# A planned kernel's orders anew: linear attention and an MLP twice, on one Trainium2 core

## The chip, the cores and the metric

The kernel runs on one core of a Trainium2 chip. Its engines are TensorE (PE, matmuls; PEld its weight loads), VectorE (DVE), ScalarE (ACT), GpSimd (POOL) and SyncE (SP, which here issues DMAs). Each works through a queue of its own in order and waits on semaphores for the others. The metric is the device time of one execution in microseconds (us), the median of some runs; smaller is better.

## The reference

The input x has 2048 rows of 512. Two layers follow each other with the same weights, and each has two parts with a residual addition:

```
x = x + A(layernorm(x))        # linear attention, 32 heads of 16
x = x + B(layernorm(x))        # MLP, 512 -> 1792 -> 512
A(x): q, k, v = x @ wqkv;  phi(t) = where(t > 0, t + 1, exp(t)) + 1e-6
      kv = sum over rows of phi(k)^T v;  z = sum over rows of phi(k)
      out = (phi(q) kv) / (phi(q) z + 1e-6) @ wo
B(x): layernorm(x); gelu(y @ w1 + b1) @ w2 + b2
```

## The kernel before, in words

The 2048 rows are 16 tiles of 128, four to a chunk. A kernel function first lists every operation as a node of a graph (`G.op`, with its engine, a duration in ns, what it reads and writes, its buffers and its name), and then plays the nodes on five queues in an order that is written out by hand as strings in `CONF`: `ORDER` names every operation of each engine in order, `PLACES` says which buffer of a pool holds which tiles one after another, `WAY` chooses the engine or the form of single operations. The durations decide nothing at run time; what runs is set by the orders and the buffers. `Settled` turns `PLACES` into dependencies (a tile's first operation waits for all users of the tile before it in the buffer) and `assign_waits` turns dependencies into semaphore waits.

The names are needed to follow the steps. The number behind a name is layer, chunk, tile:

- `statsA0_4`, `aggr`, `veps`, `pow`, `nmr`, `norm` (L783 to L811): layer norm of tile 4 ahead of the attention part of layer 0 (`A0`), or the MLP (`B0`). VectorE takes statistics (L783, L785), `veps` adds the epsilon (L790, VectorE or GpSimd), GpSimd raises to the power -0.5 (`pow`, L792), `nmr` (L803, GpSimd) is needed if ScalarE normalizes (L806); else VectorE does (L811).
- `TA0_4`, `TB0_4`: the DMA transposition of a normalized tile, issued by SP (L820). `PTA0_2`, `PTC0`: the same on TensorE (L833), whose result `tc` copies from PSUM (L843).
- `K0_4`, `Q0_1_3`: key and query matmuls (L887, L908, L920). `exp`, `relu` (ScalarE, L855, L866), `min` (VectorE, L859, L868) and `phi` (L861, L872) make the feature map from the PSUM bank. The form called "max" needs no relu, but VectorE reads the bank.
- `G0_4_0` (L997, L1026): the sum of y^T phi(k), from which `KV` (L1047) and `M` (L1070) make one matrix per layer. `zaA5`, `za5` (L971) add up phi(k) over tiles for z; `Z`, `ZH`, `ZR` are small matmuls for z; `cpg`, `cpm`, `kvm`, `zb`, `dz` copies and masks on the way.
- `D`, `pz`, `red`, `den`, `rec`, `pr`: the division. Where a chunk is treated by token, `pz` (L1112) multiplies phi(q) by z's row, `red` (L1115) sums per head, `rec` (L1120) inverts, `pr` (L1124) scales, and `TP` (L1128) transposes by DMA. `pz` and `pr` run on VectorE or GpSimd.
- `WO` (L1141) and `RA` (L1146): output matmul and residual. `b2` (L1157): addition of the bias to the residual, VectorE or GpSimd.
- `W1` with `gelu` (L1171, L1176) and `W2` with `RB` (L1208, L1214, at the end L1218, L1194 and L1200 with the stores `OD`): the MLP. In each layer's first chunk `W1` is split in two halves of 256 columns (`W10_1_5_0`, `W10_1_5_1`).

The key operations run on one chunk after another; while the MLP of layer 0 runs, norms, keys and queries of layer 1 are made for the chunks that are ready. At the start TensorE is kept running by `warm` matmuls without use, x is loaded in chunks (`x0`, `x1`, `xc1`, `xc3`, `xc2`) by SP, and the weights that are needed later (`wv`, `wo`, `w1`, `w2`) by GpSimd's queue (L730). The choices that the change touches read so:

```
on_pool = eng(f"veps{tag}") != "dve"          # L787
on_pool = eng(f"pz{tag}") != "dve"            # L1110
on_pool = eng(f"pr{tag}") == "pool"           # L1122
on_pool = eng(f"b2{L}_{st}") != "dve"         # L1156
```

Of the kernel before, what the change touches and what calls it, by code (L numbers as in the profile page):

```python
# [12 lines left out]
D = 512  # L13
# [172 lines left out]
def assign_waits(graph, order, sems, dma_sems):  # L186
# [10 lines left out]
    while len(done) < total:  # L197
        moved = False
        for e in ENGINES:
# [1180 lines left out]
```

## Time and profile before

| | |
|---|---|
| median of 3 runs | 323.85 us (323.73 to 323.98) |
| profiled execution | 325.95 us, of which the span of its instructions is 324.7 us |
| mean granted TensorE clock in the span | 0.995 |
| matmuls' busy time | PE 317.4 us |
| VectorE, ScalarE, GpSimd busy | 224.4, 190.4, 148.0 us |
| GpSimd `pow` (L792) | 64 of them, mean 666 ns |
| GpSimd `veps` (L790), `nmr` (L803) | 32 at 268 ns, 28 at 375 ns |
| GpSimd `pr` (L1124), `pz` (L1112), `b2` (L1157) | 17 at 1133 ns, 14 at 1186 ns, 9 at 1225 ns |
| VectorE `veps` (L790), `pz` (L1112), `pr` (L1124), `b2` (L1157) | 31 at 139 ns, 10 at 766 ns, 7 at 976 ns, 23 at 705 ns |
| ScalarE table loads (L1334) | 13 at 1283 ns |

The rows for VectorE and GpSimd are from the view of groups of instructions. A group by tokens (L1124) stands apart from the division by feature (L1094: 6 on GpSimd at 1161 ns, 2 on VectorE at 687 ns). Instructions of one engine overlap by some tens of ns, so an instruction's step to the next one is shorter than its duration. In a timeline the columns are start, busy time, engine, line, operation, output and inputs, shape, count, and in brackets the idle time of the engine before it and what ended it. Busy digits are tenths of slices of 8.1 us.

### The profile page before, as it was taken

How to read it: one execution, taken by the hardware profiler on the slowest of the kernel's cores; microseconds unless marked ns; L12 is line 12 of the kernel's file. 1: busy time of each engine (PE TensorE's matmuls, PEld its weight loads, DVE VectorE, ACT ScalarE, POOL GpSimd, SP SyncE). 2: the span in 40 equal slices, each digit the busy share in tenths (PEclk: the TensorE clock that was granted, in tenths of full speed). 3: DMA queues.
4: the chain of work that ended last, by engine and by line, in shares of the span. 5: the costliest groups of instructions: out<-in, count | busy, mean ns of one | idle time of the engine just before them, and what ended most of it. 6: DMA issues, size and time to landing. Idle time of an engine off the chain costs nothing.

```text
span 324.7 us, 4679 instructions
## 1 busy us (share of the span) xinstructions
PE 317.4 (98%) x1649; PEld 157.3 (48%) x1679; DVE 224.4 (69%) x541; ACT 190.4 (59%) x324; POOL 148.0 (46%) x212
## 2 busy tenths in 40 slices
PE   6999999999999999999999999999999999999997
PEld 2443445567444444444444444558644444444444
DVE  4898889999797881327279799998998894000103
ACT  3898667597660446557953478878564441663220
POOL 4789778692806642302465324976564322000000
PEclk9899999999999999999999999999999999999999
DMA  7634299314103303012201110123044233100001
GB/s 255 181 68 81 49 358 260 67 33 88 27 16 65 68 15 81 18 33 48 19 16 32 32 34 0 27 58 68 0 82 67 48 85 108 34 0 32 18 32 65
DMA packets 52355, 21.68 MB, mean 67 GB/s; under 512 B 47532, under 2 KB 50860, under 8 KB 52332
## 3 DMA queue, kind: packets, MB, share of 16 engines
q1 hardware_dynamic: 50844, 16.37, 22.7%
q0 software_dynamic: 1056, 4.72, 3.9%
q10 hardware_dynamic: 432, 0.30, 0.3%
q8 instruction: 13, 0.21, 0.3%
q14 instruction: 10, 0.08, 0.1%
HBM read 8.00 MB, written 2.10 MB: 31 GB/s over the span
## 4 chain that ended last, share of the span: by engine, by line
PE 87%; POOL 5%; DVE 4%; DMA 2%; issue 1%; ACT 0%; SPq 0%
PE ps L1171 29%; PE ps L1208 28%; PE ps L1141 9%; PE ps L920 6%; PE ps L887 5%; PE ps L1026 4%; PE ps L997 2%; POOL rstd L792 2%; POOL zacc L971 1%; DMA t<-in_A_x_dram 1%; PE ps L908 1%; PE ps L1194 1%; POOL veps L790 1%; DVE stats L783 1%; DVE yb L811 1%
## 5 line engine op out<-in xcount | busy, mean ns | idle before, releaser
L1176 ACT ACTIVATE gT<-ps,b1c 128x512 bf16<-128x512 f32 (+1 forms) x140 | 77.5, 600 | 64.2 <-PE ps L1171 63.7
L1171 PE MATMUL ps<-t,w 128*128 128x512 bf16 (+1 forms) x549 | 101.2, 336 | 0.6
L1208 PE MATMUL ps<-w,gT 128*128 128x512 bf16 x427 | 97.7, 379 | 0.4
L1171 PEld LDWEIGHTS ps<-t,w 128*128 128x128 bf16 x560 | 54.7, 98 | 43.7 <-ACT gT L1176 0.4
L1208 PEld LDWEIGHTS ps<-w,gT 128*128 128x128 bf16 x434 | 42.4, 98 | 50.6
L792 POOL TENSOR_TENSOR rstd<-veps,neghalf 128x1 f32<-128x1 f32 x64 | 42.1, 666 | 23.2 <-DVE veps L790 19.2
L855 ACT ACTIVATE eb<-ps 128x512 bf16<-128x512 f32 x62 | 35.5, 604 | 20.8 <-PE ps L887 7.8
L887 PE MATMUL ps<-wqkv,t 128*128 128x512 bf16 x128 | 33.1, 390 | 2.8 <-ACT t L843 1.8
L1218 DVE TENSOR_TENSOR yb<-ps,xsb 128x512 bf16<-128x512 f32 x15 | 10.1, 687 | 35.8 <-PE ps L1208 35.8
L783 DVE BATCH_NORM_STATS2 stats<-xsb 128x6 f32<-128x512 f32 x48 | 32.3, 684 | 0.4
L1141 PE MATMUL ps<-gtb,t 128*128 128x512 bf16 x125 | 30.7, 379 | 0.2
L806 ACT ACTIVATE yb<-xsb,nmr,rstd 128x512 bf16<-128x512 f32 x21 | 17.1, 813 | 21.1 <-POOL nmr L803 16.7
L1124 POOL TENSOR_TENSOR t<-t,rr 128x512 bf16<-128x512 bf16 x17 | 19.1, 1133 | 22.2 <-DVE rr L1120 21.8
L1214 DVE TENSOR_TENSOR xsb<-ps,xsb 128x512 f32<-128x512 f32 x16 | 10.9, 684 | 21.8 <-PE ps L1208 21.7
L866 ACT ACTIVATE rb<-ps 128x512 bf16<-128x512 f32 x43 | 25.0, 606 | 1.3 <-PE ps L908 0.8
L790 POOL TENSOR_SCALAR veps<-mv 128x1 f32<-128x1 f32 x32 | 8.6, 268 | 35.8 <-DVE mv L785 28.2
L920 PE MATMUL ps<-wqkv,t 128*128 128x512 bf16 x94 | 23.9, 379 | 0.1
L887 PEld LDWEIGHTS ps<-wqkv,t 128*128 128x128 bf16 x128 | 12.4, 100 | 19.1 <-ACT t L843 2.6
L1157 DVE TENSOR_TENSOR xsb<-xsb,b2b 128x512 f32<-128x512 f32 x23 | 15.9, 705 | 7.1 <-ACT yb L806 7.1
L1112 POOL TENSOR_TENSOR lr<-t,zrow 128x512 f32<-128x512 bf16 x14 | 16.6, 1186 | 7.4 <-ACT zrow L1010 4.2
L1141 PEld LDWEIGHTS ps<-gtb,t 128*128 128x128 bf16 x128 | 12.5, 98 | 14.5 <-ACT gtb L1010 0.2
L811 DVE TENSOR_SCALAR yb<-xsb,mv,rstd 128x512 bf16<-128x512 f32 x27 | 15.0, 563 | 6.3 <-POOL rstd L792 5.7
(99 smaller groups left out, 375.6 us busy)
## 6 DMA issues: line engine op xcount, KB each, us to landing
w<-in_B_w_dram POOLq DMA_DIRECT2D x4, 896.0 KB, 11.1
out_dram<-yb SPq DMA_DIRECT2D x15, 128.0 KB, 2.0
t<-in_A_x_dram SPq DMA_DIRECT2D x3, 512.0 KB, 4.9
t<-yb SPq DMA_TRANSPOSE x62, 2.5
wqkv<-in_A_wqkv_dram SPq DMA_DIRECT2D x1, 512.0 KB, 5.9
wqkv<-in_A_wqkv_dram POOLq DMA_DIRECT2D x1, 512.0 KB, 7.2
wo<-in_A_wo_dram POOLq DMA_DIRECT2D x1, 512.0 KB, 7.8
t<-in_A_x_dram SPq DMA_DIRECT2D x1, 384.0 KB, 4.4
```

The source lines that it names most:

```text
L783: G.op("dve", lambda e: e.bn_stats(stats[:, s.slot, :], src()), 620, reads=src_keys, writes=[k + "s"], tiles=[s, *src_tiles], name=f"stats ...
L792: G.op("pool", lambda e: e.tensor_tensor(rstd[:, s.slot:s.slot + 1], veps[:, s.slot:s.slot + 1], neghalf[:], op=ALU.pow), 570, reads=[k + ...
L811: G.op("dve", lambda e: e.tensor_scalar(yb[:, y.slot, :], src(), mean(), rstd[:, s.slot:s.slot + 1], op0=ALU.add if by_act else ALU.subtra ...
L855: G.op("act", lambda e: e.activation(eb[:, et.slot, 0:n], bank(bt, n), ACT.Exp, scale=by()), 478 if n == D else 265, reads=[src_key, *more ...
L866: G.op("act", lambda e: e.activation(rb[:, rt.slot, 0:n], bank(bt, n), ACT.Relu, scale=by()), 478 if n == D else 265, reads=[src_key, *mor ...
L887: ins = e.matmul(bank(b), lhsT=yTa(yT)[:, dt, k * P:(k + 1) * P], rhs=wqkv[:, dt, D:2 * D], start=(i == 0 and n == 0), stop=(i == len(part ...
L920: ins = e.matmul(bank(b), lhsT=yTa(yT)[:, dt, k * P:(k + 1) * P], rhs=wqkv[:, dt, 0:D], start=(dt == 0), stop=(dt == DT - 1))
L1124: lambda e, d=d, tok=tok, heads=heads: e.tensor_tensor(heads(tok()), heads(tok()), rr[:, d.slot, :].unsqueeze(2).broadcast_to([P, H, DH]), ...
L1141: ins = e.matmul(bank(wb), lhsT=yTa(pq)[:, kt, k * P:(k + 1) * P], rhs=gtb[:, kt, :], start=(kt == 0), stop=(kt == DT - 1))
L1171: ins = e.matmul(bank(b, n), lhsT=w1[:, dt, ft * P:(ft + 1) * P], rhs=yTa(yT)[:, dt, k0 * P:k1 * P], start=(dt == 0), stop=(dt == DT - 1))
L1176: G.op("act", lambda e, ft=ft, b=b, k0=k0, k1=k1, n=n: e.activation(gT[:, g.slot, ft * 512 + k0 * P:ft * 512 + k1 * P], bank(b, n), ACT.Ge ...
L1208: ins = e.matmul(bank(b), lhsT=gT[:, g.slot, ft * 512 + k * P:ft * 512 + (k + 1) * P], rhs=w2[:, ft, :], start=(ft == 0), stop=(ft == FT - 1))
```

## The change

It rewrites most of the strings in `ORDER` and `PLACES` and 50 choices in `WAY`. The operations, their number and what they compute stay the same but for the engine of these 50:

- `veps`: 12 go from GpSimd to VectorE (A0_8, A0_11, A0_12, A0_13, A0_15, A1_0, A1_2, A1_14, B0_0, B0_6, B0_14, B1_12), 11 from VectorE to GpSimd (A0_1, A1_1, A1_4, A1_7, B0_1, B0_12, B1_0, B1_3, B1_5, B1_7, B1_10).
- `pr`: pr0_2_2, pr0_3_3, pr1_0_0, pr1_2_2, pr1_3_2, pr1_3_3 go to VectorE; pr0_1_0, pr1_2_0, pr1_2_1 to GpSimd. `pz`: pz0_3_1, pz0_3_3, pz1_3_3 go to VectorE; pz1_2_0, pz1_2_3, pz1_3_0 to GpSimd.
- `b2`: b20_0, b20_2, b20_8, b20_10, b21_1, b21_4 go to VectorE; b20_1, b20_5, b20_11, b21_5, b21_7 to GpSimd. zaA5 goes to GpSimd.

A new function `load_half` (half a tile of x by its own DMA) comes in, but no entry of `LOADS` calls it; the loads, the warm-up groups and the order of the chunks stay. The core of the diff, with the first lines of each queue:

```diff
         "sp":
-            "x0 x1 wka wkc xc1 wq xc3 TA0_0 TA0_1 xc2 TA0_4 TA0_5 TA0_7 TA0_6 TA0_15 TA0_12 TA0_13 TA0_8 TA0_14 TA0_10 TA0_11 "
-            "TA0_9 b1 b2 Tb1 TP0_0_3 TP0_0_1 TP0_0_0 TP0_0_2 TB0_4 TB0_5 TB0_6 TB0_7 TB0_3 TB0_2 TP0_2_1 TB0_1 TB0_0 TP0_2_2 "
...
+            "x0 x1 wka wkc xc1 wq xc3 TA0_0 xc2 TA0_1 TA0_4 TA0_5 TA0_7 TA0_6 TA0_15 TA0_13 TA0_12 TA0_14 TA0_8 TA0_10 TA0_11 "
+            "TA0_9 b1 b2 Tb1 TP0_0_3 TP0_0_1 TP0_0_0 TP0_0_2 TB0_4 TB0_5 TB0_7 TB0_6 TB0_3 TP0_2_1 TB0_0 TB0_1 TB0_2 TP0_2_2 "
+            "TP0_2_3 TP0_2_0 TA1_4 TP0_3_2 TP0_3_0 TP0_3_1 TB0_10 TP0_3_3 TB0_8 TB0_11 TB0_9 TB0_12 TA1_5 TB0_13 TB0_15 TA1_3 "
...
         "pe":
-            "warm0 warm6 warm8 warm7 warm4 warm5 PTC0 warm2 warm1 K0_0a warm3 K0_0b K0_0c PTC1 K0_0d PTA0_2 K0_1 K0_2 Q0_0_2 "
-            "PTA0_3 G0_0_0 K0_3 Q0_0_1 Q0_0_0 G0_1_0 K0_4 G0_2_0 K0_5 G0_3_0 K0_7 Q0_1_0 K0_6 Q0_1_3 Q0_1_2 G0_4_0 G0_5_0 "
-            "K0_12 K0_15 K0_13 G0_6_0 K0_14 K0_8 K0_10 K0_11 K0_9 G0_7_0 Z0_3 Q0_0_3 G0_12_0 Z0_2 ZHA Q0_1_1 G0_13_0 D0_1_2 "
...
+            "warm0 warm5 warm1 warm4 warm8 PTC0 warm2 warm6 warm3 warm7 K0_0a K0_0b PTC1 K0_0c K0_0d PTA0_2 K0_1 K0_2 Q0_0_2 "
+            "PTA0_3 G0_0_0 K0_3 Q0_0_0 Q0_0_1 G0_1_0 K0_4 G0_2_0 K0_5 G0_3_0 K0_7 Q0_1_3 K0_6 Q0_1_0 Q0_1_2 G0_4_0 G0_5_0 "
+            "G0_6_0 K0_12 K0_13 K0_15 K0_14 K0_8 K0_10 K0_11 K0_9 Q0_0_3 Q0_1_1 G0_7_0 Z0_3 Z0_2 ZHA G0_12_0 G0_13_0 D0_1_2 "
...
+            "W10_1_10_1 W10_1_5_1 W10_1_2_1 W10_0_4_0 W10_0_13_0 W10_1_8_1 W10_0_1_0 W10_0_10_0 W10_0_5_0 W10_0_2_0 W10_1_9_1 "
...
+            "W20_6_0 W20_6_7 W10_2_3_0 W10_2_5_0 K1_4 W10_2_11_0 W10_2_10_0 W10_2_1_0 W20_7_0 W10_2_2_0 W10_2_12_0 W20_7_7 "
...
         "act":
-            "wkb wkd sumA0_3 tcC0 sqA0_3 tcC1 tcA0_2 expk0_0 reluk0_0 expk0_1 expk0_2 reluk0_1 tcA0_3 reluq0_0_2 reluk0_2 "
-            "expk0_3 reluk0_3 expq0_0_1 normA0_7 expq0_0_2 reluq0_0_0 expk0_4 reluq0_0_1 normA0_15 expk0_5 normA0_13 reluk0_5 "
...
+            "wkb wkd sumA0_3 tcC0 sqA0_3 tcC1 expk0_0 tcA0_2 reluk0_0 reluk0_1 expk0_1 expk0_2 tcA0_3 expq0_0_2 reluk0_2 "
+            "reluq0_0_2 expk0_3 normA0_7 expq0_0_0 reluk0_3 reluq0_0_1 expq0_0_1 reluq0_0_0 normA0_15 expk0_4 expk0_5 "
...
+            "gelu0_0_8_0 gelu0_0_9_0 gelu0_0_3_0 gelu0_0_7_0 gelu0_0_12_0 normB0_11 normB0_9 gelu0_2_5_0 expk1_4 gelu0_2_11_0 "
...
         "dve":
-            "ones statsA0_0 aggrA0_0 cenA0_0 statsA0_2 aggrA0_2 statsA0_1 aggrA0_1 vepsA0_1 cenA0_1 normA0_2 normA0_0 "
-            "normA0_1 statsA0_4 statsA0_5 aggrA0_4 mink0_0 aggrA0_5 normA0_3 phik0_0 statsA0_7 mink0_1 aggrA0_7 mink0_2 "
...
+            "ones statsA0_0 aggrA0_0 cenA0_0 statsA0_2 statsA0_1 aggrA0_2 aggrA0_1 cenA0_1 normA0_0 normA0_2 statsA0_4 "
+            "statsA0_5 mink0_0 aggrA0_4 normA0_3 normA0_1 aggrA0_5 phik0_0 statsA0_7 normA0_4 aggrA0_7 statsA0_6 mink0_1 "
...
-            "aggrA0_11 statsA0_9 phik0_6 phiq0_1_0 zaA5 aggrA0_9 minq0_1_2 minq0_0_0 zaA6 mink0_12 minq0_1_3 phik0_12 "
...
+            "mink0_6 aggrA0_11 phiq0_0_0 phik0_6 vepsA0_11 statsA0_9 mink0_7 minq0_1_2 minq0_1_0 minq0_1_3 phiq0_1_2 aggrA0_9 "
+            "phiq0_1_0 phik0_7 mink0_12 zaA6 normA0_9 phik0_12 mink0_13 mink0_15 phik0_13 phiq0_1_3 mink0_14 zhiA phik0_15 "
+            "mink0_8 mink0_10 phik0_10 mink0_9 mink0_11 phik0_9 phik0_11 zloA zs0_3 zs0_2 zshA zb0 dz0 minq0_1_1 minq0_0_3 "
...
+            "statsB0_7 statsB0_6 aggrB0_7 RA0_0 RA0_2 statsB0_3 RA0_1 statsB0_0 aggrB0_3 aggrB0_0 aggrB0_6 vepsB0_3 red0_2_1 "
+            "vepsB0_6 statsB0_2 minq0_2_3 statsB0_1 vepsB0_0 aggrB0_2 aggrB0_1 normB0_7 red0_2_2 normB0_6 den0_2_1 phiq0_2_3 "
+            "den0_2_2 pz0_2_0 b20_3 rec0_2_1 pr0_2_1 pz0_2_3 minq0_3_3 rec0_2_2 normB0_0 red0_2_3 normB0_1 red0_2_0 phiq0_3_3 "
+            "b20_0 RB0_5 b20_7 den0_2_0 minq0_3_0 b20_6 den0_2_3 RA0_9 minq0_3_2 statsA1_5 pz0_3_3 minq0_3_1 phiq0_3_2 "
...
         "pool":
-            "id0 bdm0 id1 neghalf vepsA0_0 powA0_0 negA0_3 vepsA0_2 powA0_2 powA0_1 vepsA0_3 bdm1 powA0_3 vepsA0_4 vepsA0_5 "
-            "powA0_4 powA0_5 vepsA0_7 powA0_7 zaA1 nmrA0_7 vepsA0_15 vepsA0_6 powA0_6 powA0_15 vepsA0_13 zaA2 nmrA0_15 "
-            "powA0_13 nmrA0_13 zaA3 vepsA0_12 powA0_12 vepsA0_8 powA0_8 vepsA0_14 nmrA0_8 vepsA0_10 powA0_14 nmrA0_14 "
-            "powA0_10 zaA4 eps6 nmrA0_10 vepsA0_11 powA0_11 nmrA0_11 vepsA0_9 powA0_9 zaA7 phik0_14 phik0_8 b1z wv wo w1_0 "
...
+            "id0 bdm0 neghalf id1 bdm1 vepsA0_0 powA0_0 negA0_3 vepsA0_2 powA0_2 vepsA0_3 vepsA0_1 powA0_3 powA0_1 b1z "
+            "vepsA0_4 powA0_4 vepsA0_5 powA0_5 vepsA0_7 powA0_7 vepsA0_6 nmrA0_7 zaA1 powA0_6 powA0_15 powA0_13 nmrA0_15 zaA2 "
+            "nmrA0_13 zaA3 vepsA0_14 powA0_12 powA0_14 vepsA0_10 nmrA0_14 powA0_8 powA0_10 nmrA0_8 nmrA0_10 zaA4 powA0_11 "
+            "nmrA0_11 zaA5 vepsA0_9 powA0_9 zaA7 phik0_14 phik0_8 eps6 wv wo w1_0 w1_1 w2_0 w2_1 phiq0_1_1 pr0_1_0 pz0_0_0 "
+            "pr0_1_3 pz0_0_1 pr0_0_3 pz0_0_2 pr0_1_1 pr0_0_1 pr0_0_0 pr0_0_2 vepsB0_4 powB0_4 vepsB0_5 powB0_5 phiq0_2_2 "
...
     WAY={
...
-        "zaA2": "pool", "zaA5": "dve", "zaA6": "dve", "zc0": "0 1",
+        "zaA2": "pool", "zaA5": "pool", "zaA6": "dve", "zc0": "0 1",
...
+        def load_half(name, queue, h, after):
+            G.parts[("x0", 0)] = (("x0", 0, 0), ("x0", 0, 1))
+            ps_ = slice(64 * h, 64 * h + 64)
+            loaded[name] = dma(queue, lambda e: e.dma_start(
+                t4[ps_, x0[0].slot, 0:D].rearrange("p (k d) -> p k d", k=1), rows(x_dram, 0)[ps_, 0:1, :]),
+                [("x0", 0, h)], [x0[0]], name=name, kb=64, after=after)
+
         for name, queue, what, at, lo, hi, behind in cf["LOADS"]:
             after = [loaded[b] for b in behind.split()]
-            if what == "x":
+            if what == "half":
+                load_half(name, queue, at, after)
+            elif what == "x":
                 load_x(name, queue, at, lo, hi, after)
```

408 rows, old and new, of tables (ORDER, PLACES, WAY) are left out of this document.

## The prediction, made before the result

> **What bounds the kernel now.** The page's first part comes first.
>
> ```profile
> PE 317.4 (98%) x1649; PEld 157.3 (48%) x1679; DVE 224.4 (69%) x541; ACT 190.4 (59%) x324; POOL 148.0 (46%) x212
> PE   6999999999999999999999999999999999999997
> ```
>
> TensorE (PE) is busy in 98% of the span; a busy PE is not PE at its peak, so I read starts instead. In PE's timeline a row's start, its count and the next row's start give the pace:
>
> ```profile
> 26.85 2.75 PE L887 MATMUL ps<-wqkv,t 128*128 128x512 bf16 x12
> 29.44 1.03 PE L997 MATMUL ps<-pkb,yb 128*128 128x512 bf16 x4
> 31.09 3.83 PE L887 MATMUL ps<-wqkv,t 128*128 128x512 bf16 x16 [0.62 <-DVE pkb L861]
> 35.22 1.02 PE L887 MATMUL ps<-wqkv,t 128*128 128x512 bf16 x4 [0.30 <-DMA t<-yb]
> 36.08 1.03 PE L997 MATMUL ps<-pkb,yb 128*128 128x512 bf16 x3
> ```
>
> Twelve matmuls take 29.44 - 26.85 = 2.59, or 0.216 each, and a group of four 0.86. The four from 29.44 take 1.65 (0.79 lost), the sixteen from 31.09 take 4.13 (0.67 lost). I went through the whole timeline so, with 0.109 for 256 columns: from 37 us to the last matmul at 322.8 one loss shows, of 0.09 at 277 (jumps of 0.21, one matmul, are missing records). So behind 37 us nothing can be won on PE and any stall is pure loss; the tail behind 322.8 (last addition and store) keeps its operations. All gain lies before 37 us. There the first real matmul starts at 6.97, behind the landing of x1 at 5.68 and ScalarE's sum and copy, and runs slowly:
>
> ```profile
> 6.97 0.61 PE L887 MATMUL ps<-wqkv,t 128*128 128x512 bf16 x1 [1.79 <-ACT t L843]
> 7.58 1.06 PE L887 MATMUL ps<-wqkv,t 128*128 128x512 bf16 x2
> 8.43 0.64 PE L833 MATMUL ps<-idp,yb 128*128 128x128 bf16 x4
> 6.97:10.38 3.41, 3.41 (x15) 1.80 (x16) 3.07 (x10) 1.66 (x4) 3.04 (x7) 0.50 0.92 320
> ```
>
> The last of these is from the view by windows: the granted clock was 0.50 from 6.97 to 10.38, so two matmuls took 0.85 instead of 0.43. Waits from 6.97 on cost, by the same count, 0.17 ahead of K0_3 (14.08), 0.79 ahead of K0_14, 0.20 ahead of K0_11, 0.46 ahead of K0_9: 1.62 us, and the slow clock about 1.6.
>
> **The start, part by part.** The end of a row is the time at which an operation can release others; between engines a release costs PE 0.24 where it waited.
>
> The half clock stays, as I take it: K0_0a still waits for the same copy (6.91). Behind it the order is K0_0a K0_0b PTC1 K0_0c K0_0d, without warm3 (0.21) between. The transposition PTC1 then ends at 8.44 instead of 9.08, its copy tcC1 at 9.06 instead of 9.70. ScalarE now runs expk0_0 before tcA0_2, so mink0_0 starts on VectorE at 10.05 and not at 11.16, where DVE's timeline shows an idle 1.05 for it. normA0_3 follows at 10.4 to 10.8 (before 11.46 to 11.85), so PTA0_3, its copy and K0_3 can come at 13.8 instead of 14.08: 0.28 won.
>
> K0_14 waited for VectorE (phik0_12 ended 31.04), and VectorE waited for GpSimd:
>
> ```profile
> 27.82 0.70 DVE L971 TENSOR_TENSOR zacc<-zacc,pkb 128x512 f32<-128x512 f32 x1 [0.58 <-POOL eps L725]
> 26.63 1.16 POOL L971 TENSOR_TENSOR zacc<-zacc,pkb 128x512 f32<-128x512 f32 x1
> 27.81 0.77 POOL L803 TENSOR_SCALAR nmr<-mv,rstd 128x1 f32<-128x1 f32 x1
> 28.93 1.07 POOL L792 TENSOR_TENSOR rstd<-veps,neghalf 128x1 f32<-128x1 f32 x1
> ```
>
> The first row is zaA5, which the change moves to GpSimd: VectorE loses 0.63 (its steps lie that far apart) and the 0.58 of waiting, and gains five veps less one at about 0.1. GpSimd gains zaA5 (1.16) and loses four net veps with their gaps (4 x 0.28 = 1.12), so its load is even, but its chain of powers starts earlier: powA0_5 at 12.4 instead of 13.34, and, with the queue walked at 0.55 to 0.6 a power, powA0_11 at 26.3 instead of 30.00 and powA0_9 at 28.8 instead of 31.39. The transposes (1.27 to issue, 1.2 to land) then put K0_11's input at 30.8 (33.76) and K0_9's at 33.0 (35.08), against turns at 32.8 and 33.7. Walking VectorE's new queue from 10.05 (stats 0.62, min 0.21, phi 0.35 or 0.60 with PSUM, norm 0.35) gives phiq0_1_2 27.9, phiq0_1_0 28.6, phik0_12 31.1, phik0_11 36.7 (before 38.41), each ahead of the PE turn that needs its bank: K0_13 28.5, K0_15 29.4, K0_10 31.9. The nearest is K0_14 behind reluq0_1_3, 29.7 against 30.2. So all of the 0.17 + 0.79 + 0.20 + 0.46 can go; with a gain of 0.28 at K0_3 that holds the first 0.17, the sum is 0.28 + 1.45, **1.7 us**; my walk gives 46.93 for KV0_0, shown at 48.70, so 1.77. Below this, 0 is the bound: none goes if something else is late there.
>
> Other edits of the start cost nothing: bdm1 (0.92) goes into GpSimd's gap between 2.68 and 4.21; xc2 is issued before TA0_1, whose reader Q0_0_1 has 1.1 to spare; pr0_1_0 on GpSimd fits into the gap before pz0_0_0, which waited for it on VectorE until 45.93; the weight loads come earlier.
>
> **Behind the start** the stream must keep this lead. Work moves both ways. VectorE gets three pr net (0.68 to 1.59, quiet row 0.69) and one b2 (0.69), pz stays ten, veps shifts; GpSimd loses three pr (1.13) and one b2 (1.22). Of these two pr, two pz and one b2 fall between 48 and 120 us: 5 x 0.69 = 3.4 us more for VectorE, which by the view by windows sat idle there for 8.5 of 72 us, 1.4 of it before 80. The tight places by the queues:
>
> (a) W10_0_4_0 now comes at 79.5, where the first such matmul came at 82.10. It needs all four TB0_0 to TB0_3. The queue of SP runs TB0_7 TB0_6 TB0_3 TP0_2_1 TB0_0 TB0_1 TB0_2 at 1.27 each; VectorE's quiet rows put normB0_0 at 74.0 and normB0_1 at 75.2, so TB0_2 lands at 79.05, 0.45 ahead, of which 0.24 is the release. Six powers are in that chain; at the mean row 666 ns instead of the quiet 550 that is 0.70 late, less 0.2 to spare: 0.5. Ends: 0, if quiet; and, below, 3.0.
>
> (b) ScalarE loads its table 15 times behind the first instead of 13 (1.28 each). At K1_4 the chain gelu, load, exp, load, gelu is 0.02 + 0.69 + 1.31 + 0.60 + 1.31 + 0.69 + 0.24 = 4.86, against PE work of 4.97 until W10_2_2_0 needs the bank. I take 0, hidden by W20_7_0; up to 0.5 if PE's work were in another order.
>
> (c) pr1_0_0 on VectorE ahead of RA1_4 makes RA1_4 0.35 late; the matmuls of the next layer's up projection had 0.85 to spare, now 0.5: 0.
>
> Sum: 1.77 - 0.5 = 1.27. Against the profiled execution (span 324.7, time 325.95, so 1.25 outside) that is 323.4 and 324.7. The plain runs stand 2.1 below it (323.73 to 323.98); that offset is carried over: 323.85 - 1.27 = 322.58, **forecast 322.6**, alone 321.9 to 323.2.
>
> **Rivals.** *The lead is spent* (0.17): VectorE or GpSimd is late at (a) by 1.3 to 2.6, or the plain runs have less of the start's waits than the profiled one; 323.2 to 324.5, say 323.8. For it: VectorE is at 7.5 of 8 us in most of 48 to 80.
>
> *The port* (0.23), slower. GpSimd's power takes 0.55 in quiet rows, but:
>
> ```profile
> 70.44 1.98 POOL L792 TENSOR_TENSOR rstd<-veps,neghalf 128x1 f32<-128x1 f32 x1
> 70.72 0.69 DVE L1124 TENSOR_TENSOR t<-t,rr 128x512 bf16<-128x512 bf16 x1
> 71.32 0.69 DVE L1157 TENSOR_TENSOR xsb<-xsb,b2b 128x512 f32<-128x512 f32 x1
> ```
>
> The power was held while two additions or products of two SBUF tensors ran on VectorE; elsewhere such a product took 1.59 and a pz 1.52 instead of 0.69. The change puts four more of them on VectorE. If in chain (a) one power is held so (1.43), one pr (0.91) and one pz (0.84), TB0_2 is 3.18 late, 2.98 beyond what is to spare: more than the lead, 323.85 + 1.2 = 325.1. From 2.6 on it decides for slower. Against it: only one power of 64 took over 1.1. [...]
>
> *The clock* (0.05): the slow 6.97 to 10.38 goes. PE was busy for 1.45 of the 3.41 us before; two more warm-up groups before K0_0a add 0.22. It would give K0_1 0.9 earlier (PTC1 then waits for cenA0_1 at 7.65): 321.4 or so. [...]
>
> **Numbers.** Forecast 0.55, clock 0.05, lead spent 0.17, port 0.23. A measurement of this kernel can tell 0.2% (0.65 us) from no change: faster 0.60, same 0.17, slower 0.23. The range 321.8 to 325.1 leaves out the clock and half of the port.
>
> **What would show it.** In the changed trace K0_3 starts near 13.8, K0_14 to K0_9 run without a gap, KV0_0 starts near 46.9, W10_0_4_0 waits under 1 us for TB0_2, and nothing else stops PE. It is wrong if zaA6 or a phi holds K0_13 to K0_10, if a power over 1 us stands in chain (a), or if PE shows gaps beyond 85 us.

## The result, and the profile after

The changed kernel took 322.75 us (median of six runs, 322.25 to 323.22) beside 323.84 for the kernel before on the same chip: ratio 0.9963, 95% interval 0.9950 to 0.9976. Twelve more runs gave 323.26 (322.19 to 324.50) beside 323.89: 0.9977, 0.9964 to 0.9990. The forecast was 322.6. (A ratio is the comparison's own figure and not the quotient of the two medians.)

The first part of the page of after, and its row by slices:

```profile
PE 315.9 (98%) x1648; PEld 156.7 (49%) x1679; DVE 224.1 (70%) x545; ACT 191.8 (60%) x326; POOL 140.4 (44%) x208
PE   7999999999999999999999999999999999999997
```

GpSimd lost 7.6 us of busy time (148.0 to 140.4), VectorE's stayed (224.4 to 224.1), PE lost 1.5 (317.4 to 315.9), mostly its rows at half pace: the second profile of after, which has such rows, shows 317.0. The shares tell nothing of where the gain is. PE's timeline does, for the stretch that lost 1.62 us in before (lines are eight higher than there):

```profile
6.20 0.60 PE L895 MATMUL ps<-wqkv,t 128*128 128x512 bf16 x2 [0.82 <-ACT t L851]
...
23.09 2.75 PE L1005 MATMUL ps<-pkb,yb 128*128 128x512 bf16 x12
25.68 7.34 PE L895 MATMUL ps<-wqkv,t 128*128 128x512 bf16 x32
32.85 1.03 PE L928 MATMUL ps<-wqkv,t 128*128 128x512 bf16 x3
```

All eight key tiles K0_12 to K0_9 are one row: 32 matmuls from 25.68 to 32.85, 7.17 us, where 32 at 0.216 take 6.91. One wait of 0.27 is left, ahead of K0_9 for the transposition of tile 9. Behind it PE loses 0.09 in the whole execution, at 274, as before does at 277. GpSimd's timeline shows one half of why; the other, the bank of K0_14, is tried below:

```profile
24.56 0.63 POOL L800 TENSOR_TENSOR rstd<-veps,neghalf 128x1 f32<-128x1 f32 x1
25.29 0.27 POOL L811 TENSOR_SCALAR nmr<-mv,rstd 128x1 f32<-128x1 f32 x1
25.51 1.16 POOL L979 TENSOR_TENSOR zacc<-zacc,pkb 128x512 f32<-128x512 f32 x1
```

The first row is powA0_11, which ended at 30.00 in before; the last is zaA5 in its new place.

Two things in this profile are not the change. The first real matmul starts at 6.20 and not at 6.97, and PE runs at full pace from 4.1 on (0.11 for 256 columns). So the profiled execution of after (322.72) stands at its plain runs, that of before stood 2.1 above them, and the two must not be subtracted. A second profile of each sorts this out; starts here are worked back from the ends of PE's operations at the pace above. Read so, K0_14 starts in before 0.23 behind the end of phik0_12 (31.04), and K0_11 and K0_9 0.30 behind the landing of their transpositions; 0.24 is taken for a release from an engine below.

| profiled kernel | x1 lands | PE at half pace from 7 to 10.4 | K0_3 | KV0_0 | time |
|---|---|---|---|---|---|
| before | 5.68 | yes | 14.08 | 48.70 | 325.95 |
| before, again | 6.00 | yes | 14.40 | 48.99 | 326.24 |
| after, again | 5.77 | yes | 13.90 | 47.25 | 324.50 |
| start of before, rest of after | 4.49 | no | 11.78 | 46.52 | 325.56 |
| after | 4.91 | no | 12.04 | 45.47 | 322.72 |
| start of after, rest of before | 4.50 | no | 11.63 | 45.45 | 322.71 |

With a late x1 the change wins 48.70 - 47.25 = 1.45 at KV0_0 (and 325.95 - 324.50 = 1.45 in time; the first joined kernel below, with x1 at 5.91, has 47.25 as well), with an early one 46.52 - 45.47 = 1.05. The plain runs won 1.09 in the first comparison and 0.63 in the second. The first fits the early kind; which kind a plain run was is not on record, as it left no trace. For before, 325.95 less 48.70 - 46.52 gives 323.77, and its plain median is 323.84.

### The profile page after: what moved, and what is told of

It is laid out like the page before. It is cut to its first block, busy times and chain, and to the rows that moved or that the text cites. A ratio compares the mean times of both kernels' runs of the same rounds, so it can differ in the third digit from the quotient of the medians.

```text
span 321.5 us, 4690 instructions
## 1 busy us (share of the span) xinstructions
PE 315.9 (98%) x1648; PEld 156.7 (49%) x1679; DVE 224.1 (70%) x545; ACT 191.8 (60%) x326; POOL 140.4 (44%) x208
## 4 chain that ended last, share of the span: by engine, by line
PE 92%; DVE 4%; ACT 1%; DMA 1%; issue 1%; POOL 0%; SPq 0%
PE ps L1179 29%; PE ps L1216 27%; PE ps L1149 9%; PE ps L895 7%; PE ps L928 6%; PE ps L1034 4%; PE ps L1005 4%; PE ps L916 2%; DMA t<-in_A_x_dram 1%; PE ps L1202 1%; DVE xsb L1165 1%; PE ps L1055 1%; PE ps L1078 1%; PE ps L1094 1%; ACT eb L863 1%
## 5 line engine op out<-in xcount | busy, mean ns | idle before, releaser
L1179 PE MATMUL ps<-t,w 128*128 128x512 bf16 (+1 forms) x550 | 102.3, 336 | 0.5
L800 POOL TENSOR_TENSOR rstd<-veps,neghalf 128x1 f32<-128x1 f32 x64 | 39.7, 631 | 28.1 <-DVE veps L798 24.2
L895 PE MATMUL ps<-wqkv,t 128*128 128x512 bf16 x127 | 31.7, 379 | 1.0 <-ACT t L851 0.8
L1149 PE MATMUL ps<-gtb,t 128*128 128x512 bf16 x123 | 30.8, 379 | 0.3
L928 PE MATMUL ps<-wqkv,t 128*128 128x512 bf16 x94 | 24.2, 379 | 0.1
L979 POOL TENSOR_TENSOR zacc<-zacc,pkb 128x512 f32<-128x512 f32 x12 | 14.5, 1210 | 11.7 <-DVE pkb L880 10.4
L1132 POOL TENSOR_TENSOR t<-t,rr 128x512 bf16<-128x512 bf16 x13 | 14.3, 1103 | 10.2 <-DVE rr L1128 9.1
```

The source lines that it names most:

```text
L800: G.op("pool", lambda e: e.tensor_tensor(rstd[:, s.slot:s.slot + 1], veps[:, s.slot:s.slot + 1], neghalf[:], op=ALU.pow), 570, reads=[k + ...
L895: ins = e.matmul(bank(b), lhsT=yTa(yT)[:, dt, k * P:(k + 1) * P], rhs=wqkv[:, dt, D:2 * D], start=(i == 0 and n == 0), stop=(i == len(part ...
L928: ins = e.matmul(bank(b), lhsT=yTa(yT)[:, dt, k * P:(k + 1) * P], rhs=wqkv[:, dt, 0:D], start=(dt == 0), stop=(dt == DT - 1))
L1149: ins = e.matmul(bank(wb), lhsT=yTa(pq)[:, kt, k * P:(k + 1) * P], rhs=gtb[:, kt, :], start=(kt == 0), stop=(kt == DT - 1))
L1179: ins = e.matmul(bank(b, n), lhsT=w1[:, dt, ft * P:(ft + 1) * P], rhs=yTa(yT)[:, dt, k0 * P:k1 * P], start=(dt == 0), stop=(dt == DT - 1))
```

## The experiments

The theory was that all of the gain is made ahead of KV0_0, by GpSimd's earlier powers and VectorE's relief, and that nothing is given back. The rivals: the gain is the clock's or x1's; it lies behind the start; GpSimd and VectorE hold each other's operations, as in the forecast's rival "port", and that takes part of it.

### The kernel before again, no edit

> The kernel before, unchanged, for a second profile and the granted clock of each of its runs. Profiled first it took 325.95 us, 2.1 above its plain runs, with a half clock from 6.97 to 10.38 us. Theory (waits): the half clock and the late landing of x1 belong to that one execution; the second profile shows clock 1.0, a span near 322.6, a time near 323.8, and still about 1.1 to 1.5 us of waits ahead of K0_14, K0_11 and K0_9. Rival (clock): the half clock is there in most runs (mean clock about 0.995 in their list), and it is what the change wins; then the second profile shows it again, and waits that are as large as in the profile after.

Measured: 323.94, ratio 1.000 (0.9983 to 1.0018). The profiled execution took 326.24, x1 landed at 6.00 and PE ran at half pace from the warm-up matmuls to 10.3, as four matmuls of 128 columns in 5.27 - 4.84 = 0.43 (0.23 in after) and two of 512 in 8.75 - 7.90 = 0.85 show:

```profile
4.84 0.63 PE L833 MATMUL ps<-idp,yb 128*128 128x128 bf16 x4
5.27 0.63 PE L751 MATMUL ps<-const-bfloat16-1.0 128*128 128x256 bf16 x2
...
7.90 1.06 PE L887 MATMUL ps<-wqkv,t 128*128 128x512 bf16 x2
8.75 0.63 PE L833 MATMUL ps<-idp,yb 128*128 128x128 bf16 x4
```

The clock column says 1.00 there, but this trace holds no record of the clock, and the column reads 1.00 for want of one: the pace is what counts. So the theory was wrong that the half pace belonged to one execution, but the rival was wrong too: at 326.24 it can't be in the plain runs at 323.9. The waits ahead of K0_14, K0_11 and K0_9 were there again with 0.78, 0.21 and 0.43.

### The kernel after again, no edit

> The kernel after, unchanged, for more plain runs and a second profile. In five profiles so far x1 landed between 4.49 and 6.00 us, though it was issued at the same time, and the first real matmul moved with it. Theory (the landing of x1 and not the kernel sets the offset between profiled and plain executions): median 322.6 to 322.9; if x1 lands behind 5.6 the profiled execution shows a half clock up to about 10.4 and stands 1.5 to 2.5 above the median, else it stands within 0.4 of it. Rival (the changed start removes the half clock for good): no half clock and no offset, whenever x1 lands.

Measured: 323.26, ratio 0.9977 (0.9964 to 0.9990). x1 landed at 5.77, and the view by windows shows the half clock in the changed kernel as well:

```profile
3.79:7.20 3.41, 1.59 (x14) 0.94 (x13) 2.04 (x7) 1.41 (x4) 1.15 (x3) 1.00 1.01 355
7.20:10.61 3.41, 3.41 (x15) 1.65 (x14) 2.97 (x9) 2.41 (x6) 2.49 (x8) 0.50 1.08 305
```

The columns are the stretch, its length, each engine's busy time, the granted clock (1.00, then 0.50) and the DMA share. The median came 0.36 above the bound of 322.9 that the theory gave, and the profiled execution stood 1.24 above it, not 1.5. The rival falls: the new start does not remove the half clock. Under "K0_14 to K0_9" this profile loses 0.19, against 1.46 in before.

### Half of the change: start of after, rest of before

The strings of each queue up to KV0_0, with their buffers and engines, are those of after; all else is that of before. The last operation of the start is `D0_1_1` on PE, `cpg0_3` on VectorE, `rec0_1_3` on ScalarE, `Tb1` on SP and `pz0_0_0` on GpSimd; the buffers' later users follow whatever the start leaves in them. Against the kernel after, PE's first line behind the joint reads:

```diff
-            "KV0_1 Q0_2_0 KV0_2 KV0_3 Q0_2_1 M0_0 Q0_2_2 M0_3 M0_2 M0_1 Q0_3_0 WO0_4_0 WO0_4_1 WO0_4_2 WO0_4_3 WO0_5_0 Q0_2_3 "
+            "KV0_1 Q0_2_0 KV0_2 KV0_3 Q0_2_1 M0_2 M0_0 Q0_2_2 M0_1 M0_3 Q0_3_0 WO0_4_0 WO0_4_1 WO0_4_2 WO0_4_3 WO0_5_0 Q0_2_3 "
...
```

> The kernel after up to about 45 us (orders, buffers and engines of everything ahead of KV0_0 and the division of chunk 0), the kernel before from there on. Theory (all of the gain is made ahead of KV0_0, and nothing is given back): 322.75 us, ratio 0.9965. Rival (the gain lies behind the start, or the start's gain is 1.77 as predicted and the rest costs 0.5 to 0.7): 323.85 by the first, 322.1 by the second.

Measured: 329.21, for a reason that has nothing to do with the question. PE and GpSimd of this kernel:

```profile
53.50 0.60 PE L1080 MATMUL ps<-wo,kvb 128*128 128x512 bf16 x2 [3.65 <-DVE kvb L1076]
```
```profile
48.70 1.15 POOL L1122 TENSOR_TENSOR lr<-t,zrow 128x512 f32<-128x512 bf16 x1 [6.89 <-DVE t L1104]
```

pr0_1_0 had come on VectorE behind cpg0_3, and pz0_0_0 on GpSimd, which needs its buffer, waited 6.89 us for it; the division of chunk 0 and then M0_2 were late. A joint between two orders must be looked through for what crosses it. Mended:

```diff
-            "... phiq0_1_1 pz0_0_0 pr0_1_3 ..."
+            "... phiq0_1_1 pr0_1_0 pz0_0_0 pr0_1_3 ..."
```

> The kernel after up to about 45 us with the rest of before again, now with pr0_1_0 on GpSimd ahead of pz0_0_0 as in after (the first such kernel put it on VectorE behind cpg0_3, so that M0_2 waited 3.8 for the division of chunk 0: a fault of the joint). Theory (all of the gain is made ahead of 45 us): 322.6 to 322.9, and no wait in the profile behind 45 us but the 0.09 at 278. Rival (the choices of engine behind 45 us are needed to keep the lead): 323.2 to 323.9, with the waits of PE between 45 and 120 us.

Measured: 322.92 (322.56 to 322.98), ratio 0.9965 (0.9953 to 0.9977), the same as after. The view of PE's waits shows two for others in the whole execution (the first row is its first warm-up matmul), and by the ends K0_9 loses the same 0.27 (and Q0_0_1, the last row, 0.39 with its release):

```profile
PE ps L761 <- PEq L1375: 0.8, 1, 0.8
PE ps L897 <- ACT t L853: 0.3, 1, 0.3
PE ps L930 <- DMA t<-yb: 0.2, 1, 0.2
```

So the gain is the start's, whole; the 42 other choices of engine (pr0_1_0 is the eighth that is kept) and all other orders behind 45 us are not needed for it.

### The other half: start of before, rest of after

> The mirror: the kernel before up to about 45 us, the kernel after from there on, with its 43 other choices of engine (three more pr, the pz, b2 and veps shifts). Theory (these cost nothing and win nothing): 323.85 us. Rival (port, or W10_0_4_0 waiting for TB0_2): with the chain to TB0_2 unchanged and the start 1.1 later nothing changes at that place either, but a shared port would show as stalls of 0.3 to 1.0 elsewhere: 324.2 to 324.9. Rival (the gain lies behind the start): 322.75.

Measured: 324.65, ratio 1.0027 (1.0008 to 1.0045): slower than before, not equal. The start lost its 0.85, 0.22 and 0.44 ahead of K0_14, K0_11 and K0_9 as before does, and PE lost 0.63 more ahead of WO0_4_2. PE, VectorE and GpSimd there:

```profile
52.60 1.47 PE L1141 MATMUL ps<-gtb,t 128*128 128x512 bf16 x6 [0.46 <-DVE gtb L1013]
```
```profile
49.92 1.23 DVE L1118 TENSOR_SCALAR rd<-rd 128x32 f32<-128x32 f32 x2
```
```profile
49.94 1.16 POOL L1094 TENSOR_TENSOR t<-t,lr 128x512 bf16<-128x512 bf16 x1
```

The second of two `den` on VectorE, 0.17 elsewhere, took 1.14, from 50.01 to 51.15, while GpSimd's pr0_1_1 ran from 49.94 to 51.11. Behind it wait red, rec and cpm0_2, and for that PE. This is a hold, as the rival "port" had it, with a price of 0.63. In after the same `den` starts at 48.62 between two operations of GpSimd (48.47 and 48.90) and takes 0.17. That after is free of it is a matter of some 0.3 us.

### One choice undone: zaA5 on VectorE

```diff
-... minq0_1_3 phiq0_1_2 aggrA0_9 ...
+... minq0_1_3 phiq0_1_2 zaA5 aggrA0_9 ...
...
-"zaA5": "pool"
+"zaA5": "dve"
```

> The kernel after with zaA5 back on VectorE, ahead of aggrA0_9, and nothing else. The prediction's step (zaA5 on GpSimd frees VectorE by 0.63 and a wait of 0.58, and that is what brings K0_14 and its followers forward): 0.6 to 1.0 us slower than after, 323.4 to 323.8. Rival (GpSimd's earlier chain of powers did it; zaA4 ends at 24.60 and VectorE reaches this place at 25.91, so there is nothing to wait for, the nearest slacks are 0.5 to 0.9, and the power of tile 9 comes 1.16 earlier and takes away the 0.27 that K0_9 still loses): 322.5 to 322.75.

Measured: 323.47 (322.73 to 325.04), ratio 0.9981 (0.9965 to 0.9997), which overlaps with both runs of after. The profile is sharper:

```profile
25.85 7.54 PE L896 MATMUL ps<-wqkv,t 128*128 128x512 bf16 x32
33.23 1.03 PE L929 MATMUL ps<-wqkv,t 128*128 128x512 bf16 x3
```

The eight key tiles take 33.23 - 25.85 = 7.38, where after takes 7.17. K0_14 starts 0.79 behind its gate reluq0_1_3, of which 0.24 is the release, K0_15 loses 0.18 behind phiq0_1_0, K0_9 loses 0.29; that makes 0.20 more than after. VectorE did not wait for zaA4, as the rival said, but the rival was wrong that the power of tile 9 would come earlier: its statistics (aggrA0_9) stand behind zaA5 on VectorE. In the trace zaA5 is worth some 0.2, not 0.6.

### Five veps undone, and the same five alone

```diff
-... powA0_6 powA0_15 powA0_13 nmrA0_15 ...
+... powA0_6 vepsA0_15 powA0_15 vepsA0_13 powA0_13 nmrA0_15 ...
...
-"vepsA0_15": "dve"
+"vepsA0_15": "pool"
```

> The kernel after with five veps (A0_8, 11, 12, 13, 15) back on GpSimd, each just ahead of its power. Theory (what cures the waits ahead of K0_11 and K0_9 is GpSimd's earlier chain of powers): 4 to 5 steps of 0.28 come back, powA0_11 ends at 26.4 instead of 25.2, powA0_9 at 28.8 instead of 27.7, the transposition of tile 9 lands near 33.0 and K0_9 loses 1.0 to 1.4 instead of 0.27: 323.6 to 324.1. Rival (the order of VectorE's queue did it, GpSimd has time): 322.6 to 323.0.

Measured: 324.38 (324.19 to 324.70), ratio 1.0008 (0.9996 to 1.0021): the whole gain gone, more than expected. powA0_11 ended at 27.34 and powA0_9 at 29.77. PE lost 0.32 ahead of K0_6, 0.98 ahead of K0_13, 0.18 at K0_14 and K0_8 and 0.34 ahead of K0_9. PE's and VectorE's timelines:

```profile
27.78 5.53 PE L896 MATMUL ps<-wqkv,t 128*128 128x512 bf16 x24 [0.81 <-DVE t L870]
```
```profile
19.27 1.38 DVE L881 TENSOR_TENSOR t<-eb,rb 128x512 bf16<-128x512 bf16 x1
```

By the order of the queues, the lateness reaches PE by more ways than the power of tile 9: ScalarE's norms wait for the powers and its exponentials stand behind them, VectorE's minima wait for those. And a phi of 0.42 was held to 1.38 by zaA3 (19.12 to 20.36 on GpSimd).

```diff
-... aggrA0_15 normA0_5 aggrA0_6 statsA0_13 ...
+... aggrA0_15 vepsA0_15 normA0_5 aggrA0_6 statsA0_13 ...
...
-"vepsA0_15": "pool"
+"vepsA0_15": "dve"
```

> The kernel before with these five veps on VectorE, each just behind its aggr, and nothing else. Theory: GpSimd's powers of tiles 11 and 9 end about 0.9 to 1.1 earlier and zaA4 with them, VectorE pays 0.65 for five veps and gets back up to 0.58 of its wait for zaA4; so the wait ahead of K0_9 (0.44) goes, that ahead of K0_14 (0.80, behind VectorE's phik0_12) stays: 323.2 to 323.6. Rival (the veps alone bring all of it): 322.6 to 322.9. Rival (VectorE only gets later): 323.9 to 324.4.

Measured: 325.82 (325.00 to 327.06), ratio 1.0050 (1.0036 to 1.0065). The waits ahead of K0_11 and K0_9 went, as the theory said, and that ahead of K0_14 stayed with 0.71. But 1.62 came up ahead of Q0_1_0, which no theory had. PE, VectorE and GpSimd:

```profile
21.94 1.04 PE L908 MATMUL ps<-t,wqkv 128*128 128x512 bf16 x4 [1.44 <-DVE pkb L861]
```
```profile
16.28 1.38 DVE L872 TENSOR_TENSOR pkb<-eb,rb 128x512 bf16<-128x512 bf16 x1
...
18.78 1.15 DVE L859 TENSOR_SCALAR eb<-eb 128x512 bf16<-128x512 bf16 x1
```
```profile
16.08 1.29 POOL L971 TENSOR_TENSOR zacc<-zacc,pkb 128x512 f32<-128x512 f32 x1
...
18.62 1.16 POOL L971 TENSOR_TENSOR zacc<-zacc,pkb 128x512 f32<-128x512 f32 x1
```

Each row of VectorE (0.42 and 0.28 elsewhere) began just behind the start of an addition on GpSimd and ended 0.15 to 0.29 behind its end: 0.96 and 0.87 lost, by a shift of some tenths. The five veps need the order that goes with them.

### Two buffers exchanged: the bank of K0_14

```diff
-"psum_4": "... k0_6 k0_12 k0_10 q0_1_1 ..."
-"psum_7": "... q0_1_3 k0_14 k0_11 zc0_3 ..."
+"psum_4": "... k0_6 k0_12 k0_14 k0_11 zc0_3 ..."
+"psum_7": "... q0_1_3 k0_10 q0_1_1 ..."
```

> The kernel after with two PSUM buffers' successors exchanged: K0_14 and K0_11 follow K0_12 in its bank (as they do in before), K0_10 and Q0_1_1 follow Q0_1_3. No order and no engine changes. Theory (the 0.80 ahead of K0_14 went because its bank now comes free by ScalarE's reluq0_1_3 and no longer by VectorE's phik0_12): K0_14's turn is 28.44, phik0_12 ends at 29.19, a release takes 0.24, so 0.8 to 1.0 comes back there, of which the 0.27 ahead of K0_9 takes up some: 323.3 to 323.9, at a place that neither zaA5 nor the five veps touch. Rival (VectorE and GpSimd are early enough with any buffers): 322.5 to 322.9 and no wait at K0_14.

Measured: 323.88 (323.04 to 324.65), ratio 0.9993 (0.9976 to 1.0009). PE's timeline:

```profile
29.31 4.49 PE L895 MATMUL ps<-wqkv,t 128*128 128x512 bf16 x20 [0.82 <-DVE pkb L869]
```

By the ends, K0_14 lost 0.99 behind phik0_12 (29.26) and K0_9 no longer lost its 0.27: as the theory had it. So with the new VectorE order and the new powers, the wait ahead of K0_14 would still be there in the old bank.

### TA0_1 and xc2 in the old order

```diff
-            "x0 x1 wka wkc xc1 wq xc3 TA0_0 xc2 TA0_1 TA0_4 ..."
+            "x0 x1 wka wkc xc1 wq xc3 TA0_0 TA0_1 xc2 TA0_4 ..."
```

> The kernel after with TA0_1 ahead of the load xc2 in SP's queue, as in before. The prediction had this order cost nothing (1.1 to spare at Q0_0_1). In two profiles in which x1 landed early (4.41, 4.50) Q0_0_1 lost 0.34 and 0.39 behind TA0_1, which took 2.6 from the end of its issue to landing, beside xc2; in before it took 1.5. Theory (xc2 ahead of it makes TA0_1 late): TA0_1 lands by 12.2, nothing is lost at Q0_0_1, 322.4 to 322.7. Rival (TA0_1 is late because its norm ends at 9.6, two us later than in before, and the place of xc2 does nothing): 322.7 to 323.0, with 0.1 to 0.4 at Q0_0_1 still if x1 lands early.

Measured: 323.54 (322.61 to 323.93), ratio 0.9976 (0.9958 to 0.9993). The theory was right on TA0_1 (landed at 12.23, nothing lost at Q0_0_1), but the median did not follow, and PE shows why one tile later:

```profile
15.73 1.02 PE L895 MATMUL ps<-wqkv,t 128*128 128x512 bf16 x4 [0.68 <-DMA t<-yb]
```

Now TA0_4 ran beside xc2 (landed at 15.02), took from 12.87 to 15.60 to land, and K0_4 lost 0.84. One transposition of the two pays for the 512 KB: with x1 at 4.5, Q0_0_1 lost 0.39 in after's order (start of after) and K0_4 0.84 in this one. The medians (323.54 beside 322.75 and 323.26 of after) do not tell the two orders apart.

### Two tries for a better version

```diff
-            "wkb wkd sumA0_3 tcC0 sqA0_3 tcC1 ..."
+            "wkb wkd tcC0 sumA0_3 sqA0_3 tcC1 ..."
```

> The kernel after with tcC0 ahead of sumA0_3 on ScalarE, so that the first real matmul no longer waits for x1. Theory (the half clock of some executions comes of TensorE's idle time until x1 lands): K0_0a starts at 5.9 to 6.1 whenever x1 lands, no profile and no plain run shows a half clock, the plain runs lie closer together (322.2 to 323.0) with a median of 322.4 to 322.7; PTC1, which waits for VectorE's cenA0_1, takes back what an early K0_0a wins when x1 is early. Rival (the clock goes by something else): a spread of 322.2 to 324.5 as before. Rival (sumA0_3 0.6 later delays normA0_3 and K0_3): 323.0 to 323.4.

Measured: 323.00 (322.84 to 323.31), ratio 0.9965 (0.9950 to 0.9979). x1 landed as late as 5.56 here, and there was no half clock behind 7 us. PE's timeline:

```profile
5.94 0.60 PE L895 MATMUL ps<-wqkv,t 128*128 128x512 bf16 x2 [0.20 <-ACT t L851]
7.54 0.40 PE L841 MATMUL ps<-idp,yb 128*128 128x128 bf16 x4 [0.99 <-DVE yb L805]
```

The matmul no longer waits for x1; PTC1, which needs tile 1 of x1, does. The twelve runs lie within 0.47, those of after within 2.31. The median is not better than after's, the highest is by 1.2.

```diff
-['wkd', 'act', 'wk', 0, 3, 4, ''], ['wkc', 'sp', 'wk', 0, 1, 2, '']
+['wkd', 'act', 'wk', 0, 3, 4, 'x0'], ['wkc', 'sp', 'wk', 0, 1, 2, 'x0']
```

> The kernel after with tcC0 ahead of sumA0_3 as in the run before, and two of the four loads of key weights, wkd and wkc (128 KB each), held back until x0 has landed (3.2 us), so that x1 (384 KB) shares the DMA engines with less. Aimed at a version that beats both kernels. Theory (what moves x1's landing between 4.4 and 6.0 is the weight traffic beside it, and the start behind x1 sets the end): x1 lands by 4.7, wkd and wkc by 6.8 (K0_0c and K0_0d then wait up to 0.3), K0_1 starts by 8.2, plain runs at 322.2 to 322.8 with a median of 322.5. Rival (x1's landing goes by something else): x1 lands between 4.4 and 6.0, median 322.9 to 323.3 as without it. Rival (the weights or the later loads of x come too late): 323.3 to 324, with waits at K0_0c, K0_0d or K0_4.

Measured: 323.19, ratio 0.9973 (0.9959 to 0.9987). x1 landed at 4.50, but in one profile, and it did so in others without this edit: not told apart. The wait of the third case came true, K0_0c waited for its weights, though the time lies in the range of the second:

```profile
7.35 0.60 PE L895 MATMUL ps<-wqkv,t 128*128 128x512 bf16 x2 [0.48 <-DMA wqkv<-in_A_wqkv_dram]
```

No version here beats after by more than the spread.

## Why the forecast held, point by point

**The start, 1.77: right in its working, too large for the plain runs.** The walk assumed a late x1 and the half clock; the second profile of after is such an execution. Predicted and measured there:

| | predicted | measured |
|---|---|---|
| mink0_0 starts, normA0_3 ends | 10.05, 10.8 | 10.02, 10.70 |
| K0_3 starts | 13.8 | 13.90 |
| powA0_11, powA0_9 end | 26.3, 28.8 | 26.75, 29.56 |
| TA0_11, TA0_9 land | 30.8, 33.0 | 31.32, 33.64 |
| phiq0_1_2, phik0_12, phik0_11 end | 27.9, 31.1, 36.7 | 27.80, 31.05, 36.89 |
| KV0_0 starts | 46.93 | 47.25 |

The sum there is 1.45: 0.18 at K0_3 (0.28 predicted) and 0.80 + 0.20 + 0.46 less 0.19 that K0_9 still waits. The missed size is the transposition of tile 9: its power came 0.76 later, and it landed 1.97 behind the end of its issue (31.67 to 33.64) where 1.2 was taken. Why is open: tile 9 took 1.86 to 2.05 in nine profiles with the start of after, but 1.20 in all with the start of before and when the bank of K0_14 was exchanged. With an early x1 little is left of the gain at K0_3 (11.78 to 11.63 with x1 at 4.50; with x1 at 4.91 K0_3 started at 12.04), and the sum is 1.05.

**"xc2 ahead of TA0_1 costs nothing": true with a late x1 only.** The prediction gave Q0_0_1 1.1 to spare. With x1 at 4.50 (start of after) TA0_1 landed at 13.44, beside xc2, and Q0_0_1 lost 0.39. So an x1 that lands before 4.9 wins nothing in after: K0_3 started 0.41 earlier there, KV0_0 at 45.45 beside 45.47.

**The step "zaA5 frees VectorE" carried too much.** Undone alone it costs 0.2 in the trace. What brought K0_14 forward is its bank, which now waits for ScalarE's reluq0_1_3 (0.99 when undone), and what brought the rest forward is the chain of powers without five veps (1.1 to 1.6 when undone). The prediction had the bank (it took reluq0_1_3 as K0_14's gate) without saying that it was new, and that it was needed.

**(a), 0.5: not paid.** TB0_2 landed at 76.86, W10_0_4_0 started at 78.00, 1.14 behind, and waited for nothing. In the other profile of after it was 78.64 and 79.78. The six powers of the chain took 0.54 to 0.79, 3.85 in all, where six at the feared 0.666 make 4.00; normB0_0 and normB0_1 were earlier than the walk had them (73.52 and 74.57 in the profile with the late x1, for 74.0 and 75.2).

**(b) and (c): right.** W10_2_2_0 had 0.34 from its gelu to its start, of which 0.24 is the release: 0.10 to spare, where 0.11 was worked out. W11_1_8_0 started 0.75 behind TB1_5: 0.51 to spare, where 0.5 was worked out.

**The offset of 2.1, carried over: wrong as a rule, harmless here.** It was x1's landing and the half pace of one profiled execution. 1.27 was the difference of a start that came out smaller (1.05 for 1.77) and a wait that did not come (0 for 0.5): 0.72 too much and 0.5 too much taken off, so the forecast came within 0.15 of the first six runs in part because two errors met, which is luck. The twelve later runs, at 323.26, lie 0.66 above it, just outside the 321.9 to 323.2 that it gave itself.

**The rivals.** The lead was not spent behind the start: the kernel with before's rest is as fast. The half clock behind 7 us did not change with the kernel: both have it in all four profiles in which x1 landed at 5.68 or later, and none of the ten others shows it. Of the rival "port" the runs show the holds, and nothing of a port: a hold decided in a start of before with the rest of after (0.63), and in the five veps alone two held operations stand ahead of the wait of 1.62. In after none decided anything.

## What to carry to other kernels

Before two profiled executions are subtracted, their first input's landing and TensorE's pace up to 10.4 us have to be the same; here these alone moved 2 us. A wait of TensorE for a key tile had two gates close together (K0_11 in the start of before: its bank, freed at 31.66, and its transposition, landed at 31.60), and the one part of the change that was tried alone, the five veps, won nothing: list the second gate of every stall before pricing an edit. The orders of VectorE and GpSimd were worth as much as their relative timing, some tenths of a us (a `den` took 0.17 in after and 1.14 in the start of before with the rest of after), and an edit that only shifts one queue must be walked against the other's long operations.

## What the hardware showed besides

**VectorE waits out operations of GpSimd, in 205 cases.** In 14 profiles I took every VectorE operation that began while GpSimd had over 0.35 us left of a 128x512 tensor operation. Those with two SBUF tensors (`pr`, `pz`, `b2`, phi without PSUM: 97) and the scalar forms on SBUF `min` (59) and `den` (26) were all held, for the rest of GpSimd's operation less 0.13 us; so were all 23 of `norm`, less 0.26. Of the 1105 others, those with a PSUM operand, the statistics, the reductions, `rec` and the 128x1 steps, none was. Before has 15 held of 91 such operations, after 15 of 100: a `pz` that began at 84.15 in before, with 0.98 left on GpSimd, took 1.53 where 0.69 is usual; a `den` at 76.32 in after, with 1.11 left, 1.15 for 0.17; a phi from PSUM at 28.50 in after, with 1.10 left, its usual 0.69. Why VectorE waits there no run shows. The prediction had priced a held power, pr and pz; what was held ahead of PE's waits here were `den`, `min` and phi.

**The half clock followed stretches in which TensorE was partly busy.** In before it lasted 3.41 us (6.97 to 10.38). In the 3.41 us ahead of it PE was busy for 1.45, 1.59, 1.55 and 1.27 us, 37 to 47% (before, after again, and twice in the first joined kernel, the second time up to 54.77, behind the wait of 3.65). In the second profile of before the pace was half at 4.84 already, and up to 10.3. Whether the busy time decides, and from what share on, was not tried; in the run with tcC0 ahead, PE went to full pace at 5.2 and kept it through the 3.41 us from 5.27, with 2.17 us busy.

**Landings scatter.** x1, issued at 1.25 in every profile, landed between 4.41 and 6.00; a transposition landed 1.2 us behind the end of its issue at best, 1.2 to 2.05 for tile 9, and up to 3.7 while the first loads still ran (TA0_0 in the last try, 8.05 to 11.77). That after's plain runs scatter over 2.3 us, while most of before's lie within 0.6, goes with it: the waits that before has at 32 to 36 us would take up a late start, after has none left. This is argued from the profiles and was not tried.
